# Clustered attention before two expert layers: cluster products on four column tiles, one assignment for both halves, the output halves added on GpSimd

## The chip, the core and the metric

One core of one Trainium2 chip. The metric is the device time of one execution in microseconds. TensorE (PE), VectorE (DVE), ScalarE (ACT) and GpSimd (POOL) run their own queues of instructions in order; SyncE (SP) issues most DMAs, one after another.

## The reference

Attention over 2 batches, 8 heads, 768 tokens and 64 channels, in which a query sees only the keys of its own cluster; then a layer of eight experts (1,536 tokens, 512 to 1024 to 512 channels), then a gated layer (512 to 1536 to 512).

```python
q_n = q / (np.linalg.norm(q, axis=-1, keepdims=True) + 1e-06)
c_n = centroids / (np.linalg.norm(centroids, axis=-1, keepdims=True) + 1e-06)
q_assign = np.argmax(np.einsum('bhsd,hcd->bhsc', q_n, c_n), axis=-1)
...
mask = q_assign[:, :, :, None] == k_assign[:, :, None, :]
scores = np.where(mask, scale * np.matmul(q, k.transpose(0, 1, 3, 2)), -1000000000.0)
attn = np.exp(scores - np.max(scores, axis=-1, keepdims=True))
attn = attn / (np.sum(attn, axis=-1, keepdims=True) + 1e-09)
return np.matmul(attn, v)
```

With 16 clusters, each token of q and k gets the first cluster with the largest product (the norm of the token changes no order). The change touches attention alone.

## The kernel before, in words

**Pairs and steps.** The 16 heads are taken as 8 pairs (two heads side by side in 128 partitions, 64 channels each). `Attention.run` walks 96 steps `g`, twelve to a pair; a step is 128 queries of one head against its 768 keys. The list `CFG["order"]` says in what order a step issues its parts: `E` (`evac`, in every third step: copy the finished output accumulator out), `S` (`soft`, the exponential of the next step), `Q` (`qk`, the score products of the step after that, and VectorE's maximum of them), `T0` and `T1` (`pt`: each three transposes of the exponentials, a ScalarE cast to the high part, a VectorE subtraction for the low part), `B0` (the first background part that falls to this step), `O` (`onat`, output products of a finished half), `V0` and `V1` (`pv`, two matmuls each on the high and two on the low parts into `acc`), `B1` (the other background parts). So on TensorE a step begins with the score products of two steps later. PSUM tiles: `s` and `t` have two buffers, `acc` and `mm` one; everything in the background and the output products share `mm`.

**Numbers in float32 precision.** The score products use float32r and split operands: q and k are transposed, cast to a high part H, the rest is a low part L (GpSimd or VectorE), and X = H + L is the exact value. SP moves H and L into the tiles A and B that the products read (`moves`, L181). The tiles B hold, beside the parts, 16 rows per head in which the one-hot cluster of each token stands, for the keys scaled by a large number, so that the score product itself adds the mask.

**The background of a pair.** While pair n-1 runs, pair n is prepared. `prep_steps` names the parts and `CFG["offs"]` (for the first prepared pair `CFG["offs1"]`) gives each a step, counted from the start of pair n-1; parts of one step keep the order of the list. Negative numbers lie in the pair before. Step 8: q0, 9: k0, 10: q1, 0: k1 (transposes `tr`, and behind the second half the moves), then the loads of the next pair. Step 2: v1, a0q. Step 3: a0k. Step 4: v0. Step 6: a1q, a1k, f0, f1. Step 7: m0, m1. The output products fall to steps 1 and 5, `evac` to steps 0, 3, 6 and 9.

**Assignment** (`assign`, L193; `first`, L219; for the first pair `assign0`). For each half of the tokens and each of q and k, three plain float32 matmuls have 128 tokens of X as the stationary operand and the 32 columns of two heads' centroids (`cbd`) as the moving one (L205); each appears in the trace as two records. When both are there, VectorE takes the maximum over the 16 clusters (L214), compares (L215), GpSimd multiplies by descending ranks (L216), and `first` takes the maximum of that and compares again (L226, L227): a one-hot of the first best cluster, tokens in partitions.

**Mask** (`mask`, L256). For each half the one-hot (128 x 64) is transposed by three matmuls (L266), ScalarE scales it into `oT` (64 rows: q and k of two heads, L280), and after the second half SP moves four blocks of 16 rows x 768 tokens into `qB` and `kB` (L131).

**Copy-out** (`evac`, L383). `acc` holds the product with V's high part in its lower 64 partitions and with V's low part in the upper ones: ScalarE copies the upper half (L391), VectorE adds it to the lower one into `O` (L393). The last pair takes its heads in another order, and its output product is in the same step as the copy-out.

Of the kernel before, what the change touches and what calls it, by code (L numbers as in the profile page):

```python
# [23 lines left out]
class Attention:  # L24


    def __init__(self, tc, ctx, q, k, v, cent, gate, x, lg, ident, raw):
# [23 lines left out]
        self.desc = one.tile([128, J * 2, C], F32, name="desc")  # L51
        self.sc = one.tile([4 * C, 2], F32, name="sc")
# [4 lines left out]
    def fixed(self):  # L57

        nc, C = self.nc, self.C
        nc.gpsimd.memset(self.cbd, 0.0)  # L60
        nc.gpsimd.memset(self.sc[0:2 * C, 0:1], 1.0)
        nc.gpsimd.memset(self.sc[0:2 * C, 1:2], 0.0)
        nc.gpsimd.memset(self.sc[2 * C:4 * C, 0:1], NEG)
        nc.gpsimd.memset(self.sc[2 * C:4 * C, 1:2], -NEG)
        nc.gpsimd.iota(self.desc, pattern=[[0, self.J * 2], [-1, C]], base=C, channel_multiplier=0,
                       allow_small_or_imprecise_dtypes=True)
        for t in self.qB + self.kB:
            nc.gpsimd.memset(t[0:64, 1, :].bitcast(F32), 0.0)
# [124 lines left out]
    def assign(self, n, half, si):  # L193
        nc, st = self.nc, self.pairs[n]
        J, C = self.J, self.C
        HJ = J // 2
        b, hp = divmod(n, self.H // 2)
        if si == 0:
            if half == 0:
                st["oh"] = self.one.tile([128, J, 4, C], F32, name="oh")  # L200
            st["ps"] = self.ps_m.tile([128, HJ, 4, C], F32, tag="mm", name="asp")
        ps = st["ps"]
# [5 lines left out]
        if si == 0:  # L208
            return
        G = HJ * 4  # L210
        psf = ps.rearrange("p j s c -> p (j s) c")
        mx = self.p2.tile([128, G], F32, name="mx")
        eq = self.p2.tile([128, G, C], F32, name="eq")
# [3 lines left out]
        st["eq", half] = eq  # L217

    def first(self, n, half):  # L219
        nc, st = self.nc, self.pairs[n]  # L220
        J, C = self.J, self.C
        HJ = J // 2
        G = HJ * 4
        eq = st.pop(("eq", half))
        m2 = self.p2.tile([128, G], F32, name="m2")
# [4 lines left out]
    def assign0(self, si):  # L230
# [3 lines left out]
        G = J * 2  # L234
# [961 lines left out]
```

## Time and profile before

| | |
|---|---|
| time, median of 3 runs | 815.84 us (815.63 to 816.18) |
| the profiled execution's own time | 816.51 us |
| its span, first to last instruction | 814.8 us |
| TensorE busy, granted clock | 786.3 us (97% of the span), 0.993 of full speed |
| VectorE, ScalarE, GpSimd busy | 597.6, 397.8, 263.3 us |
| attention's steps | from 15.35 us (first score product) to about 277 us |

The span leaves out 1.7 us around the first and the last instruction. Busy shares are averages over attention, experts and the gated layer, which have different limits: in attention VectorE and ScalarE are much busier than over the whole span, so the change is read from attention's own stretch. In timelines a row starts with its start and its duration in us; neighbouring instructions of one kind are one row (x2, x6), and records of one engine can overlap.

### The profile page before, as it was taken

Reading aid. Unit: us, or ns where it says so; the run is one execution under the profiler, and the core shown is the slowest. Engines: PE = TensorE matmul, PEld = TensorE weight load, DVE = VectorE, ACT = ScalarE, POOL = GpSimd, SP = SyncE. Lnnn points to the kernel's source line nnn. Section 1 sums busy time; section 2 is a strip of 40 time slices with the busy share of each in tenths; the row PEclk is TensorE's granted clock in tenths of the full one; section 3 lists DMA queues with packets and bytes.
Section 4 is the critical chain, followed back from the end, with each engine's and each line's share of the span. In section 5 each row is a group of like instructions: output and inputs, shape, how many; then the busy total and the mean of one; then the engine's idle time right before and its main releaser. Section 6 shows DMA issues by size and latency. Waiting matters only on the chain. (4 is left out here: it accounts for less than half of the span.)

```text
span 814.8 us, 13168 instructions
## 1 busy us (share of the span) xinstructions
PE 786.3 (97%) x4903; PEld 710.6 (87%) x4903; DVE 597.6 (73%) x995; ACT 397.8 (49%) x757; POOL 263.3 (32%) x283
## 2 busy tenths in 40 slices
PE   7999999999999889999999999999999999999996
PEld 6999999998989779999999988778888888888885
DVE  5899999999999757666565643678877777777433
ACT  5797887887988544455444532233322222212210
POOL 6322222322221285000000011566545445444234
PEclk9899999999999999999999999999999999999999
DMA  9855957725531166666664641322122121210012
GB/s 203 212 124 149 231 162 210 175 59 128 127 102 69 60 238 197 206 209 213 221 218 154 200 155 30 100 77 91 65 78 78 52 76 54 78 53 0 1 52 103
DMA packets 93316, 102.06 MB, mean 125 GB/s; under 512 B 30304, under 2 KB 77408, under 8 KB 93248
## 3 DMA queue, kind: packets, MB, share of 16 engines
q1 hardware_dynamic: 88384, 89.33, 38.3%
q0 software_dynamic: 1920, 6.29, 2.0%
q10 hardware_dynamic: 2944, 5.54, 1.9%
q8 instruction: 42, 0.69, 0.3%
q14 instruction: 26, 0.21, 0.1%
HBM read 68.21 MB, written 12.58 MB: 99 GB/s over the span
## 5 line engine op out<-in xcount | busy, mean ns | idle before, releaser
L366 DVE TENSOR_TENSOR PTl<-t,PTh 128x384 fp32r<-128x384 f32 x192 | 98.1, 548 | 6.2 <-ACT PTh L365 5.3
L1003 POOL TENSOR_TENSOR cm<-raw 128x512 f32<-128x512 f32 x36 | 47.8, 1329 | 155.6 <-DMA raw<-in_moe_w_gate 153.6
L365 ACT CAST PTh<-t 128x384 fp32r<-128x384 f32 x192 | 83.7, 491 | 27.6 <-PE t L363 27.3
L337 DVE TENSOR_REDUCE nm<-s 128x1 f32<-128x768 f32 x96 | 91.2, 951 | 6.7 <-PE s L334 5.7
L347 ACT ACTIVATE P<-s,nm 128x768 f32<-128x768 f32 x96 | 87.8, 914 | 2.7 <-DVE nm L337 1.7
L363 PE MATMUL t<-ident,P 128*128 128x128 f32 x576 | 83.2, 278 | 0.8 <-DVE PTl L366 0.7
L363 PEld LDWEIGHTS t<-ident,P 128*128 128x128 f32 x576 | 68.2, 142 | 9.7 <-DVE PTl L366 3.9
L380 PE MATMUL acc<-PTh,V 128*128 128x384 f32 x192 | 73.0, 380 | 1.3 <-DVE O L393 1.2
L841 PE MATMUL yp<-Hhh,W2h 128*128 128x256 f32 x256 | 73.1, 285 | 0.0
L1048 POOL TENSOR_TENSOR ghl<-u,ghh 128x512 fp32r<-128x512 f32 x36 | 49.8, 1384 | 71.4 <-ACT ghh L1047 71.4
L841 PE MATMUL hp<-Xl,W1h 128*128 128x256 f32 x256 | 72.6, 283 | 0.3 <-DVE Xl L834 0.3
L841 PE MATMUL hp<-Xh,W1h 128*128 128x256 f32 x256 | 72.6, 283 | 0.3 <-ACT Xh L833 0.3
L841 PE MATMUL yp<-Hhh,W2l 128*128 128x256 f32 x256 | 72.5, 283 | 0.0
L841 PE MATMUL yp<-Hhl,W2h 128*128 128x256 f32 x256 | 72.4, 283 | 0.0
L841 PE MATMUL hp<-Xh,W1l 128*128 128x256 f32 x256 | 72.4, 283 | 0.0
L380 PE MATMUL acc<-PTl,V 128*128 128x384 f32 x192 | 64.6, 337 | 0.0
L1045 DVE TENSOR_TENSOR u<-sg,g 128x512 f32<-128x512 f32 x36 | 24.8, 688 | 52.1 <-ACT sg L1044 52.1
L1067 DVE TENSOR_TENSOR acc<-o,acc 128x512 f32<-128x512 f32 x60 | 40.4, 690 | 19.7 <-PE o L1059 19.7
L334 PE MATMUL s<-Ak,Aq 128*128 128x384 f32 x192 | 52.6, 355 | 1.4 <-ACT P L347 1.4
L1047 ACT CAST ghh<-u 128x512 fp32r<-128x512 f32 x36 | 22.4, 621 | 64.3 <-DVE u L1046 64.3
L334 PE MATMUL s<-kB,qB 80*128 80x384 f32 (+1 forms) x192 | 50.7, 345 | 0.9 <-ACT kB L272 0.7
L808 DVE TENSOR_TENSOR W2l<-raw,W2h 128x1024 fp32r<-128x1024 f32 x32 | 40.0, 1249 | 15.1 <-ACT W2h L807 14.4
(268 smaller groups left out, 2137.9 us busy)
## 6 DMA issues: line engine op xcount, KB each, us to landing
raw<-in_moe_w SPq DMA_DIRECT2D x64, 512.0 KB, 4.4
Ak<-Hk SPq DMA_DIRECT2D x32, 192.0 KB, 4.9
moe_rows<-zero SPq DMA_DIRECT2D x8, 768.0 KB, 6.0
raw<-in_moe_w_gate SPq DMA_DIRECT2D x12, 512.0 KB, 3.6
raw<-in_moe_w_val SPq DMA_DIRECT2D x12, 512.0 KB, 3.6
raw<-in_moe_w_out SPq DMA_DIRECT2D x12, 512.0 KB, 3.5
xr<-moe_rows ACTq DMA_DIRECT2D x7, 768.0 KB, 6.4
ldq<-in_q SPq DMA_DIRECT2D x16, 192.0 KB, 4.2
```

Of the source, the lines that this page charges most:

```text
L334: nc.tensor.matmul(ps[:, c, 0:HS], lhsT=ql[:, qs], rhs=kr[:, c * HS:(c + 1) * HS], start=a == 0, stop=a == 1)
L337: nc.vector.tensor_reduce(out=nm, in_=ps[:, :, 0:HS], axis=AX.XY, op=ALU.max, negate=True)
L347: nc.scalar.activation(out=P, in_=ps[:, :, 0:HS], func=AF.Exp, bias=nm, accum_out=self.pairs[n]["sum"][:, i, r:r + 1])
L363: nc.tensor.transpose(ps[:, jj, :], P[:, a, jj * 128:(jj + 1) * 128], self.ident)
L365: nc.scalar.copy(out=Ph[:, js, cs], in_=ps)
L366: nc.vector.tensor_tensor(out=Pl[:, js, cs], in0=ps, in1=Ph[:, js, cs].bitcast(F32), op=ALU.subtract)
L380: nc.tensor.matmul(hs["acc"], lhsT=V[:, j, :], rhs=m[:, j, :], start=(j == 0 and a == 0), stop=(j == self.J - 1 and a == 1))
L808: nc.vector.tensor_tensor(out=l, in0=t, in1=h.bitcast(F32), op=ALU.subtract)
L841: self.nc.tensor.matmul(out, lhsT=W[a][:, k, cols], rhs=mov[b][:, k, :], start=i == 0, stop=i == n - 1)
L1003: self.nc.gpsimd.tensor_tensor(out=m, in0=Hw, in1=Hw, op=ALU.mult)
L1048: nc.gpsimd.tensor_tensor(out=hl[:, fc], in0=u, in1=hh[:, fc].bitcast(F32), op=ALU.subtract)
L1067: nc.vector.tensor_tensor(out=a, in0=p[t], in1=a, op=ALU.add)
```

## The change

The 12 cluster products of a pair become four: the centroids (32 columns) are stationary, 384 tokens of X move, and the four products (two halves, q and k) go to four column tiles of 32, so that their results stand in four blocks of 32 partitions of one PSUM tile (`assign`). ScalarE copies that to SBUF, and a new part `pick` transposes it by three matmuls back to tokens in partitions, where both halves are assigned at once (384 columns instead of twice 192). `mask` transposes the one-hot of both halves by three matmuls, one activation scales it, and eight moves of 16 rows x 384 tokens take it to B. The new tiles lie in the buffers of others (`as` in that of Lq, `eqa` in that of Lk). The parts a0q, a0k, a1q, a1k, f0, f1, m0, m1 become a, t, f, m, at steps 2, 3, 5, 7 (first prepared pair: 3, 4, 5, 6). In `evac` ScalarE copies both halves of the accumulator and GpSimd adds them. The ranks are kept once and broadcast; the first pair's own mask is now `mask0`.

```diff
-    def assign(self, n, half, si):
+    def assign(self, n):
...
-        for jj in range(HJ):
-            j = half * HJ + jj
-            nc.tensor.matmul(ps[:, jj, 2 * si:2 * si + 2].rearrange("p r c -> p (r c)"),
-                             lhsT=st["X" + "qk"[si]][:, j * 128:(j + 1) * 128], rhs=self.cbd[:, hp, :],
-                             start=True, stop=True)
...
+        ps = self.ps_m.tile([128, HS], F32, tag="mm", name="asp")
+        for half in range(2):
+            for si, nm in enumerate("qk"):
+                g = (2 * half + si) * 2 * C
+                nc.tensor.matmul(ps[g:g + 2 * C], lhsT=self.cbd[:, hp, :], rhs=st["X" + nm][:, half * HS:(half + 1) * HS],
+                                 start=True, stop=True, tile_position=(0, g))
+        st["as"] = self.one.tile([128, HS], F32, tag="Lq", name="as")
+        nc.scalar.copy(out=st["as"], in_=ps)
+
+    def pick(self, n):
...
+        ps = self.ps_m.tile([128, HJ, 128], F32, tag="mm", name="ast")
         for jj in range(HJ):
+            nc.tensor.transpose(ps[:, jj, :], st["as"][:, jj * 128:(jj + 1) * 128], self.ident)
+        G = HJ * 8
...
+        mx = self.one.tile([128, G], F32, name="mxa")
+        eq = self.one.tile([128, G, C], F32, tag="Lk", name="eqa")
         nc.vector.tensor_reduce(out=mx, in_=psf, axis=AX.X, op=ALU.max)
         nc.vector.tensor_tensor(out=eq, in0=psf, in1=mx.unsqueeze(2).to_broadcast([128, G, C]), op=ALU.is_equal)
-        nc.gpsimd.tensor_tensor(out=eq, in0=eq, in1=self.desc, op=ALU.mult)
+        nc.gpsimd.tensor_tensor(out=eq, in0=eq, in1=self.desc.to_broadcast([128, G, C]), op=ALU.mult)
...
+    def mask(self, n):
+        nc, st = self.nc, self.pairs[n]
+        C, HJ, HS = self.C, self.J // 2, self.S // 2
+        oT = self.one.tile([128, HS], F32R, tag="oT", name="oT")
+        ps = self.ps_m.tile([128, HJ, 128], F32, tag="mm", name="otp")
+        for jj in range(HJ):
+            nc.tensor.transpose(ps[:, jj, :], st["oh"][:, jj, :], self.ident)
+        nc.scalar.activation(out=oT, in_=ps.rearrange("p j t -> p (j t)"), func=AF.Identity, scale=self.sc[:, 0:1],
+                             bias=self.sc[:, 1:2])
+        for half in range(2):
+            sl = slice(half * HS, (half + 1) * HS)
+            for si, nm in enumerate("qk"):
                 Bt = st["B" + nm]
-                r0 = 2 * si * C
-                if n:
-                    self.move(Bt[64:64 + C, 0], st["oT"][r0:r0 + C])
-                self.move(Bt[64 - C:64, 1], st["oT"][r0 + C:r0 + 2 * C])
+                r0 = (2 * half + si) * 2 * C
+                self.move(Bt[64:64 + C, 0, sl], oT[r0:r0 + C])
+                self.move(Bt[64 - C:64, 1, sl], oT[r0 + C:r0 + 2 * C])
...
-        ol = self.one.tile([D, HS], F32, tag="ol", name="ol")
-        nc.scalar.copy(out=ol, in_=acc[D:2 * D])
-        o = self.pairs[n]["O"][r * D:(r + 1) * D, half * HS:(half + 1) * HS]
-        nc.vector.tensor_tensor(out=o, in0=acc[0:D], in1=ol, op=ALU.add)
+        rows = slice(r * D, (r + 1) * D)
+        ol = self.one.tile([2 * D, HS], F32, tag="ol", name="ol")
+        o = self.pairs[n]["O"][rows, half * HS:(half + 1) * HS]
+        nc.scalar.copy(out=o, in_=acc[0:D])
+        nc.scalar.copy(out=ol[rows], in_=acc[D:2 * D])
+        nc.gpsimd.tensor_tensor(out=o, in0=o, in1=ol[rows], op=ALU.add)
```

## Rows read from the trace of the kernel before

The pair shown is the fourth in order of time; its steps begin, on TensorE, at 110.58 (step 10 of the pair before it, by the score products that are two steps ahead), 112.99 (11), 115.05 (0), 117.58 (1), 120.49 (2), 123.13 (3), 125.95 (4), 128.02 (5), 130.83 (6), 134.15 (7), 137.65 (8), 140.12 (9), and 142.68 begins the next step 10.

**Rows 1.** Busy us (instructions) by stage: PE, PEld, DVE, ACT, POOL; clock, DMA, GB/s.
```profile
110.58:142.68 32.10, 31.66 (x223) 30.17 (x223) 29.98 (x60) 26.24 (x61) 8.19 (x10) 1.00 0.69 191
110.58:120.49 9.91, 9.91 (x70) 9.38 (x70) 9.34 (x17) 9.77 (x24) 3.02 (x3) 1.00 0.57 124
120.49:123.13 2.64, 2.64 (x21) 2.60 (x21) 2.50 (x8) 1.54 (x5) 0.35 (x1) 1.00 1.02 357
123.13:137.65 14.52, 14.08 (x102) 13.37 (x102) 13.60 (x29) 10.23 (x23) 3.80 (x6) 1.00 0.88 259
137.65:142.68 5.03, 5.03 (x37) 4.81 (x35) 4.55 (x9) 4.69 (x11) 1.00 (x1) 1.00 0.20 41
```

**Rows 2.** Timeline of TensorE: steps 11 and 0 begin, step 7's mask transposes.
```profile
112.99 0.52 PE L334 MATMUL s<-Ak,Aq 128*128 128x384 f32 x2
...
115.05 0.51 PE L334 MATMUL s<-Ak,Aq 128*128 128x384 f32 x2
...
136.13 0.49 PE L266 MATMUL otp<-ident,oh 128*64 128x128 f32 x3 [0.38 <-DVE oh L227]
```

**Rows 3.** Two source lines: duration ns min/median/max, first and last start.
```profile
L205 PE MATMUL asp<-cbd,Xq x84: 192/276/276, 29.1 to 230.2; 128*128 128x32 f32 x84
...
L410 PE MATMUL on<-R,O x96: 286/286/390, 54.8 to 280.2; 128*128 128x144 f32 x96
```

**Rows 4.** Groups, 30 to 320 us: busy us, mean ns | idle us before.
```profile
L366 DVE TENSOR_TENSOR PTl<-t,PTh 128x384 fp32r<-128x384 f32 x186 | 94.8, 548 | 5.6 <-ACT PTh L365 5.0
...
L337 DVE TENSOR_REDUCE nm<-s 128x1 f32<-128x768 f32 x90 | 85.6, 951 | 3.9 <-PE s L334 2.9
...
L347 ACT ACTIVATE P<-s,nm 128x768 f32<-128x768 f32 x91 | 83.3, 915 | 2.5 <-DVE nm L337 1.5
...
L391 ACT COPY ol<-acc 64x384 f32<-64x384 f32 x32 | 15.2, 477 | 10.7 <-PE acc L380 10.0 <-ACT x L662 0.2
...
L393 DVE TENSOR_TENSOR O<-acc,ol 64x384 f32<-64x384 f32 x32 | 17.5, 547 | 0.7 <-ACT ol L391 0.2
...
L280 ACT ACTIVATE oT<-otp,sc 64x384 fp32r<-64x384 f32 x14 | 9.4, 669 | 6.1 <-PE otp L266 6.1
...
L214 DVE TENSOR_REDUCE mx<-asp 128x12 f32<-128x192 f32 x14 | 5.0, 354 | 1.2 <-PE asp L205 1.0
...
L157 POOL TENSOR_TENSOR Lk<-Xk,Hk 128x384 fp32r<-128x384 f32 x12 | 12.0, 1003 | 25.9 <-ACT Xk L156 25.9
```

**Rows 5.** Timeline of ScalarE in step 3 and of VectorE in step 5.
```profile
124.45 0.86 ACT L365 CAST PTh<-t 128x384 fp32r<-128x384 f32 x2 [0.15 <-PE t L363]
...
130.73 0.16 DVE L405 TENSOR_SCALAR rs<-sum 128x6 f32<-128x6 f32 x1
...
131.82 0.54 DVE L393 TENSOR_TENSOR O<-acc,ol 64x384 f32<-64x384 f32 x1
```

**Rows 6.** Timeline of SP's DMA issues, two pairs.
```profile
124.86 0.60 SPq L131 DMA_DIRECT2D kB<-Lk  x1
...
138.63 1.22 SPq L131 DMA_DIRECT2D qB<-oT  x2
139.90 1.22 SPq L131 DMA_DIRECT2D kB<-oT  x2
...
238.26 1.22 SPq L131 DMA_DIRECT2D kB<-oT  x2
```

**Rows 7.** DMA issues by line: count, KB each, us from issue to landing.
```profile
kB<-Lk SPq DMA_DIRECT2D x16, 192.0 KB, 4.4
...
kB<-oT SPq DMA_DIRECT2D x15, 48.0 KB, 2.1
```

**Rows 8.** Timeline of TensorE: first score products of a new pair.
```profile
143.03 0.52 PE L334 MATMUL s<-kB,qB 80*128 80x384 f32 x2
...
239.87 0.51 PE L334 MATMUL s<-Ak,Aq 128*128 128x384 f32 x2
...
240.49 0.59 PE L334 MATMUL s<-kB,qB 80*128 80x384 f32 x2
```

More of the change, by code (lines that the diff above doesn't have):

```diff
@@ L50, in __init__ @@
         self.cbd = one.tile([128, H // 2, 2 * C], F32, name="cbd")
[L51 to L52 removed]
+        self.desc = one.tile([128, 1, C], F32, name="desc")
+        self.sc = one.tile([8 * C, 2], F32, name="sc")
         self.pairs = {}
@@ L214, in assign, with first @@
         nc.vector.tensor_reduce(out=mx, in_=psf, axis=AX.X, op=ALU.max)
         nc.vector.tensor_tensor(out=eq, in0=psf, in1=mx.unsqueeze(2).to_broadcast([128, G, C]), op=ALU.is_equal)
-        nc.gpsimd.tensor_tensor(out=eq, in0=eq, in1=self.desc, op=ALU.mult)
-        st["eq", half] = eq
-    def first(self, n, half):
+        nc.gpsimd.tensor_tensor(out=eq, in0=eq, in1=self.desc.to_broadcast([128, G, C]), op=ALU.mult)
+        st["eq"] = eq
+    def first(self, n):
         nc, st = self.nc, self.pairs[n]
[L221 to L225, printed above, removed]
+        C, HJ = self.C, self.J // 2
+        G = HJ * 8
+        eq = st.pop("eq")
+        m2 = self.one.tile([128, G], F32, name="m2a")
@@ L226, in first @@
         nc.vector.tensor_reduce(out=m2, in_=eq, axis=AX.X, op=ALU.max)
-        nc.vector.tensor_tensor(out=st["oh"][:, half * HJ:(half + 1) * HJ].rearrange("p j s c -> p (j s) c"), in0=eq,
+        st["oh"] = self.one.tile([128, HJ, 128], F32, tag="oh", name="oh")
+        nc.vector.tensor_tensor(out=st["oh"].rearrange("p j (g c) -> p (j g) c", c=C), in0=eq,
                                 in1=m2.unsqueeze(2).to_broadcast([128, G, C]), op=ALU.is_equal)
@@ L236, in assign0 @@
         if si == 0:
-            st["oh"] = self.one.tile([128, J, 4, C], F32, name="oh")
+            st["oh"] = self.one.tile([128, J, 4, C], F32, tag="oh", name="oh")
         pt = self.ps_t.tile([128, J // 2, 128], F32, tag="t", name="t")
@@ L254, in assign0, with mask0 @@
                         op=ALU.is_equal)
-    def mask(self, n, half):
-        nc, st = self.nc, self.pairs[n]
+    def mask0(self, half):
+        nc, st = self.nc, self.pairs[0]
         J, C, S = self.J, self.C, self.S
@@ new lines, in mask0 @@
+        nc.scalar.activation(out=st["Bk"][64:64 + C, 0, sl], in_=flat[2 * C:3 * C], func=AF.Identity,
+                             scale=self.sc[2 * C:3 * C, 0:1], bias=self.sc[2 * C:3 * C, 1:2])
+        self.late.append((sl, flat))
+        for sl, flat in self.late if half else ():
+            nc.vector.tensor_copy(st["oT"][q, sl], flat[q])
+            nc.scalar.activation(out=st["oT"][k, sl], in_=flat[k], func=AF.Identity, scale=self.sc[k, 0:1],
+                                 bias=self.sc[k, 1:2])
@@ L454, in run @@
         self.warm(self.ps_m, "mm", 28)
-        self.mask(0, 0)
-        self.mask(0, 1)
+        self.mask0(0)
+        self.mask0(1)
         self.vsplit(0, 0)
```

54 lines of the change are left out of this document (18 added, 36 removed).

## The prediction, made before the changed kernel ran

> **What bounds the kernel now.** I read the busy time by stage first, then TensorE's order of work, then the other engines' durations, last the DMA issues of SP. Attention runs in twelve steps to a pair of heads; seven of the eight pairs carry the preparation of the next pair, and only that preparation and the copy-out of the output change. The first view [rows 1] cuts one such pair (32.10 us) at its steps: steps 10, 11, 0 and 1 take 9.91, step 2 takes 2.64, steps 3 to 7 take 14.52, steps 8 and 9 take 5.03. TensorE is busy in 31.66 of the 32.10, VectorE in 29.98, ScalarE in 26.24, GpSimd in 8.19. So TensorE sets the pair, with VectorE close behind, and from step 8 to step 1 ScalarE too (4.69 + 9.77 of 14.94). A step without preparation takes 2.06 us, from one score product's start to the next [rows 2]. Twelve of those are 24.7 us; the other 7.4 are preparation, output products and waits. One wait is plain: in step 7 the transposes of the mask wait 0.38 us for VectorE's one-hot [rows 2].
>
> **The cluster products.** Before, a pair issues 24 records (two per product, 12 products, 128x32): 6 in step 2, which is why that step takes 0.58 more than a plain one, 6 in step 3 and 12 in step 6; some 2.4 us in all. After, it issues 8 records of 384 columns, all in step 2. Their price follows from two rows [rows 3]: a plain f32 record lasts 192 ns at its shortest with 32 columns and 286 with 144, so a column costs 94/112 = 0.84 ns (two cycles at the granted 2.4 GHz), and 384 columns stream for 0.32 us. No row has column tiles, so the sum has two ends: all 8 one behind the other are 8 x 0.32 = 2.6 us, and four tiles fully side by side are 2 x 0.32 = 0.64 us. Both records of a product need the same 32 columns of the array and have to follow each other; the program issues tile 0 twice, tile 1 twice and so on. If TensorE starts records in their order, the second record of one tile can run with the first of the next, and no more: five slots, 1.6 us. I take 1.7, with 0.1 for going in and out of the tiles. It lies between the ends, since the records of this trace all keep their order, which excludes the lower end, and the upper one would need the tiles to do nothing. The Trainium skill (TensorEngine Tiling (Array Packing), Key Properties) says that different tiles run their matmuls in parallel, but also that a change of tiling mode drains the engine; by the first alone the products would take 0.64 us, which is a rival below.
>
> Step 2 so goes from 2.64 to 2.06 + 1.7 = 3.76: **+1.1**.
>
> **Steps 3 to 7.** TensorE loses 18 records of products (6 in step 3, 12 in step 6) and 3 of 6 mask transposes, and gains 3 transposes of the copied scores in step 3 (128 columns, 0.11 each). Its own work there is then five plain steps, 0.33 for scores, 0.33 for the mask and 0.73 for one output product (6 records of 0.12): 11.7 us. VectorE loses two output additions (547 ns each), and its assignment turns from two sets of 192 columns into one of 384: a reduction goes from 354 ns to about 0.55 (between the 354 of 192 and the 951 of 768 columns), a 384-wide operation takes 548 [rows 4]; start to start the four come to 2.05 us, where the eight old ones took about 2.8. ScalarE loses one mask activation (669), and gains the score copy (about 0.48) and a second output copy for each group of three steps (477) [rows 4]. GpSimd's product with the descending ranks and its output sum are about 1.0 us each, as its 384-wide subtraction [rows 4]; with 24 idle us in a pair it hides both. The sum waits for ScalarE's copies; behind it in GpSimd's queue stand k's low part (step 0) and the product with the ranks (step 3), each some 1 us later and read a step later; the output products read the sum a step or more after it, but for the last pair.
>
> What counts is the order. The products end with step 2, so the score copy waits at the head of ScalarE's queue until then, and behind it are the two output copies and the exponential that step 4 needs. From the start of step 3: score copy 0.2 to 0.65, output copies to 1.6, exponential to 2.5 (915 ns), casts from 2.5. Before, the casts began at 1.3 (124.45 [rows 5], less 123.13). VectorE's first subtraction follows the cast by 0.5, at 3.0 instead of 1.9. From there its queue is nearly full: two subtractions to 4.0, maximum and equality to 5.05, step 4 to 6.85 (a plain step costs it 1.85, one maximum of scores and two subtractions, neighbours overlapping), step 5 to 8.65, the one-hot to 9.6, the output scaling to 10.7 (1.09, from its first record to the group after it [rows 5]), step 6's subtractions to 12.4. The transposes write a PSUM tile of two buffers, so those of step 7 can't start before step 6's subtractions release them, at 12.0 and 12.45; with mask transposes and output accumulation step 7 ends at 13.8 instead of 14.52: **-0.7**. The 2.1 us between this and TensorE's own 11.7 are new waits for VectorE; the old one for the one-hot is gone.
>
> One more wait can arise: the equality now writes into the buffer of Lk, whose last move is issued at 124.86 [rows 6] and lands 4.4 us later [rows 7], at about 129.3. In the new order the equality runs at 123.13 + 1.1 + 4.5 = 128.7. That is 0.6 at most, in the pairs whose queue also carries zero fills; I take it at nothing and keep it for the range.
>
> **Steps 8 to 1.** The accumulator is released by two ScalarE copies instead of a copy and an addition queued on VectorE; I give back 0.25 for the waits in steps 9 and 0. ScalarE gets 0.95 more work against 0.48 idle; the other 0.5 is hidden while TensorE waits in step 10 for the mask, and would show without that wait. That wait is the price. Before, SP issued four moves of the mask from 138.63 on, 0.63 apart [rows 6], and they land 2.1 us after issue [rows 7]; the third, issued at 139.90, lands at 142.0, and the product that reads it starts at 143.03 [rows 8]: 1.0 of slack. In a later pair the third is issued at 238.26 [rows 6], so lands at 240.4, and the product starts at 240.49, 0.62 behind its forerunner, where 0.35 is usual [rows 8]; so this wait exists already. After, there are eight moves of half the size, and the keys of the first head are complete only with the seventh. No row shows an issue get shorter with its rows, so I keep 0.63 for each: four issues or 2.54 us later. (Behind the moves SP has only those of q in step 10, which come free later than that.) Against it stand 0.68 (with one activation the first issue comes about 0.3 after step 8 begins, not 0.98), the slack of 1.0 and 0.18 because only the second matmul needs the seventh move: 0.7, and 0.85 as steps 8 and 9 are themselves 0.15 faster. Bounds: 0 if a half-size move issues in 0.4, 1.5 if the product waits for all eight. **+0.6** net.
>
> **The sum.** A middle pair: 1.1 - 0.7 + 0.6 = +1.0; six of them, +6.0. The first prepares its mask a step earlier and has no wait for it: +0.2. The last has no preparation and a relieved VectorE, but its one output product in the copy-out's own step now waits for two copies and a GpSimd sum: +0.3. Start-up and experts see nothing: four more small memsets and a shorter iota lie under the first loads. The profiled execution takes 816.51 us, 0.67 above the median; 816.51 + 6.5 - 0.67 = **822.3 us**.
>
> **Rivals.** (a) VectorE's relief decides: it loses about 2.9 us a pair, and if the lead of the score products covers its bursts in steps 3 and 5, a pair falls to TensorE's work, 24.7 + 1.3 + 1.5 for unchanged transposes and output products, 0.66 and 1.7 for the new ones, 29.9, plus the wait for the mask: 30.75. That is -1.35 in six pairs and some -2.4 for first and last: 805. The high busy share of VectorE speaks for it, the late casts of step 3 against; it decides if steps 4 to 7 hold no TensorE gap over 0.2 us. Chance 0.25. (b) Tiles truly side by side: 0.75 for the products, 0.95 less a pair, 815.7, no change. No row shows two records side by side. Chance 0.2. The Trainium skill stands on both sides (TensorE: Matmul & The Clock Gate, Part 3): it measured 2.38 times for three column tiles, yet calls matmuls strictly in order, as my five slots do; no run here shows either for tiles. (c) The tiles don't overlap at all, so the change doesn't do what it says: 2.7 for the products, 829. All matmul records here stream one by one. Chance 0.2. My case has 0.35.
>
> **Numbers.** Less than 0.2% (1.6 us) can't be told from no change here. Faster: (a) and a little of (b), 0.28. Same: half of (b) and an edge of mine, 0.14. Slower: 0.58. The range goes from 808, inside (a), to 829, the middle of (c); it leaves out the far half of each, about 0.2.
>
> **What would show it.** Right: 8 product records spread over some 1.6 us at the end of step 2; casts of step 3 about a microsecond later; TensorE waiting for subtractions in steps 4 to 7; a gap of 0.5 to 1.0 before the mask's second key product in step 10, ended by a move into kB. Wrong: a middle pair under 31.5 us, no gap in step 10, or products that take 0.7 or 2.6.

## The result, and the profile after the change

| | before | after |
|---|---|---|
| time, median | 816.63 us (815.63 to 817.91, 7 runs) | 827.22 us (822.19 to 828.22, 7 runs) |
| ratio | | 1.0107, 95% interval 1.0081 to 1.0134 |
| profiled execution, span | 816.51, 814.8 us | 824.82, 822.8 us |
| granted clock in it | 0.993 | 0.991 |
| first to 96th score product | 250.8 us | 257.2 us |

The change is slower, by 10.6 us in the medians (1.1%, with an interval clear of 1). Part of that is the clock: the granted clock differs between executions, and 4 of the 7 runs of after had 0.986 or 0.987. The one run of after at 0.996 took 822.19; three runs of before at 0.996, from all comparisons, took 815.29 to 815.52. So at equal clock the difference is 6.8 us, as far as one run of after can tell. In the two profiles it lies in attention's steps (6.4), in the stretch from the last score product to the first expert product, in which the last output products and the router stand (31.65 us after 31.07; below: the tail), and in TensorE's clock at start-up. After that the time is the same (517.5 us before and 517.3 after, from the first expert product to the end).

The clock at start-up belongs to the execution: in this profile of after TensorE was granted half its clock (1.2 of 2.4 GHz) for 3.41 us from 10.05 us, in the middle of nearly unbroken transposes and products, and its first score product came at 16.59 us; in the nine profiles of kernels below that have no such stretch it came at 15.25 to 15.66, as before the change (15.35), and in the three that have it at 16.27 to 16.42. A second such stretch, of 6.83 us, lies in the first pair, from 18.89 us before and from 20.29 after. So the comparisons below use **A**, the time from the 13th to the 96th score product, behind both: 219.72 us before, 226.62 after (its ends in after are the rows at 47.18 and 273.80 of the TensorE fence below). A pair is named by its place in order; the fourth is the one of [rows 1].

The fourth pair of after, by the same stages as [rows 1] (all, steps 10 to 1, 2, 3 to 7, 8 and 9; columns as there):

```profile
112.20:145.18 32.98, 31.34 (x208) 27.41 (x208) 27.33 (x50) 28.40 (x65) 11.94 (x14) 1.00 0.67 185
...
112.20:122.90 10.70, 10.21 (x69) 9.39 (x69) 8.63 (x15) 10.32 (x26) 4.53 (x5) 1.00 0.59 134
...
122.90:125.83 2.93, 2.93 (x23) 2.03 (x22) 2.79 (x9) 1.61 (x4) 0.56 (x2) 1.00 0.97 321
...
125.83:140.38 14.55, 13.40 (x86) 11.27 (x83) 12.28 (x25) 11.82 (x26) 5.40 (x6) 1.00 0.86 248
...
140.38:145.18 4.80, 4.80 (x36) 4.72 (x36) 3.63 (x6) 4.65 (x11) 1.45 (x2) 1.00 0.11 26
```

TensorE now has 15 records fewer, VectorE is 2.65 us less busy, ScalarE 2.2 and GpSimd 3.75 us more; and yet the pair is 0.88 longer, because TensorE idles for 1.64 us where it idled for 0.44. The stages say where: steps 10 to 1 take 0.79 more, step 2 takes 0.29 more, steps 3 to 7 the same, steps 8 and 9 take 0.23 less.

TensorE's timeline in after (start, duration, count, idle before): the wait in step 10, the products at the end of step 2, the wait in step 5, the last score product, the last pair's output product behind it.

```profile
47.18 0.52 PE L348 MATMUL s<-Ak,Aq 128*128 128x384 f32 x2
...
113.40 0.44 PE L348 MATMUL s<-kB,qB 80*128 80x384 f32 x1 [0.49 <-DMA kB<-oT]
...
124.78 0.34 PE L394 MATMUL acc<-PTl,V 128*128 128x384 f32 x1
125.05 0.51 PE L203 MATMUL asp<-Xq,cbd 128*32 128x384 f32 x1
125.06 0.51 PE L203 MATMUL asp<-Xk,cbd 128*32 128x384 f32 x1
125.06 0.51 PE L203 MATMUL asp<-Xq,cbd 128*32 128x384 f32 x1
125.07 0.51 PE L203 MATMUL asp<-Xk,cbd 128*32 128x384 f32 x1
125.40 0.49 PE L203 MATMUL asp<-Xq,cbd 128*32 128x384 f32 x1
...
125.42 0.49 PE L203 MATMUL asp<-Xk,cbd 128*32 128x384 f32 x1
125.83 0.62 PE L348 MATMUL s<-Ak,Aq 128*128 128x384 f32 x2
...
132.78 1.01 PE L377 MATMUL t<-ident,P 128*128 128x128 f32 x6 [0.85 <-DVE PTl L380]
...
273.80 0.52 PE L348 MATMUL s<-Ak,Aq 128*128 128x384 f32 x2
...
276.82 1.00 PE L426 MATMUL on<-R,O 128*128 128x144 f32 x6 [1.30 <-POOL O L409]
```

**The products run side by side.** The first records of all four tiles start within 0.02 us, the four second ones 0.35 later. From 124.96, where the next record would have followed (0.18 behind 124.78, as its neighbours), to the score product at 125.83 the four products cost TensorE 0.87 us. The column of the last record streams until about 125.74 (an estimate: 0.32 us for 384 columns, as in the prediction), so some 0.09 us are lost on the way into the tiles and 0.09 on the way out.

**ScalarE and VectorE in step 3**, which begins at 125.83 (timelines of after, ScalarE first):

```profile
126.01 0.48 ACT L206 COPY as<-asp 128x384 f32<-128x384 f32 x1 [1.02 <-PE asp L203]
126.52 0.47 ACT L407 COPY O<-acc 64x384 f32<-64x384 f32 x1
127.01 0.47 ACT L408 COPY ol<-acc 64x384 f32<-64x384 f32 x1
127.51 0.90 ACT L361 ACTIVATE P<-s,nm 128x768 f32<-128x768 f32 x1
...
128.40 0.85 ACT L379 CAST PTh<-t 128x384 fp32r<-128x384 f32 x2
```

```profile
128.90 1.02 DVE L380 TENSOR_TENSOR PTl<-t,PTh 128x384 fp32r<-128x384 f32 x2 [1.10 <-ACT PTh L379]
129.84 0.55 DVE L218 TENSOR_REDUCE mxa<-ast 128x24 f32<-128x384 f32 x1
130.84 0.56 DVE L219 TENSOR_TENSOR eqa<-ast,mxa 128x384 f32<-128x384 f32 x1 [0.45 <-DMA kB<-Lk]
131.32 0.94 DVE L351 TENSOR_REDUCE nm<-s 128x1 f32<-128x768 f32 x1
132.18 1.01 DVE L380 TENSOR_TENSOR PTl<-t,PTh 128x384 fp32r<-128x384 f32 x2
```

ScalarE idles 1.02 us for the products and then has two copies and an exponential ahead of the casts, which begin 2.57 us into the step. VectorE idles 1.10 us for them, then does its two subtractions, the maximum, waits 0.45 us for a move that still reads Lk, and is late with step 4's subtractions, for which TensorE waits 0.85 us in step 5.

**SP's mask moves** ahead of the same pair's step 10 (timeline of SP, then the profile's DMA list with count, KB each and us to landing):

```profile
107.68 1.22 SPq L132 DMA_DIRECT2D qB<-oT  x2
108.95 1.22 SPq L132 DMA_DIRECT2D kB<-oT  x2
110.21 1.22 SPq L132 DMA_DIRECT2D qB<-oT  x2
111.48 1.22 SPq L132 DMA_DIRECT2D kB<-oT  x2
```

```profile
kB<-oT SPq DMA_DIRECT2D x28, 24.0 KB, 1.9
```

A move of half the size still takes 0.63 us to issue. The seventh of the eight is issued at 111.48, and its reader starts at 113.40, 1.9 us later.

Summed over the pairs, the steps read: first pair -0.5, six middle pairs +5.13 (193.42 to 198.55), last pair +1.77 (26.30 to 28.07), tail +0.58: +7.0 in all. The six middle pairs are not alike: +0.2 in the second and the sixth, +0.7 and +0.9 in the third and the fourth, +1.3 in the fifth, +1.8 in the seventh. The seventh is taken up at kernels 4 and 5. In the fifth, one pair of move issues ahead of step 10 took 0.7 us more than any other in this profile:

```profile
142.04 1.94 SPq L132 DMA_DIRECT2D kB<-oT  x2
```

Step 10 waited 1.36 us there and lasted 4.04, against 3.1 to 3.3 in the fifth pairs of kernels 2, 3, 4 and 6, which wait for the same eight moves in the same order. So some 0.8 us of A in after belong to this one execution.

### The profile page after: what moved, and what is told of

It is laid out like the page before. It is cut to its first block, busy times and chain, and to the rows that moved or that the text cites. A ratio compares the mean times of both kernels' runs of the same rounds, so it can differ in the third digit from the quotient of the medians.

```text
span 822.8 us, 12991 instructions
## 1 busy us (share of the span) xinstructions
PE 785.7 (95%) x4791; PEld 693.4 (84%) x4791; DVE 577.2 (70%) x935; ACT 413.1 (50%) x789; POOL 293.2 (36%) x312
## 5 line engine op out<-in xcount | busy, mean ns | idle before, releaser
L377 PE MATMUL t<-ident,P 128*128 128x128 f32 x576 | 86.8, 282 | 7.4 <-DVE PTl L380 7.2
L409 POOL TENSOR_TENSOR O<-O,ol 64x384 f32<-64x384 f32 x32 | 32.2, 1006 | 55.3 <-ACT ol L408 53.3
```

Source lines behind the costliest of these rows:

```text
L377: nc.tensor.transpose(ps[:, jj, :], P[:, a, jj * 128:(jj + 1) * 128], self.ident)
```

## The experiments

Each kernel is after or before with the edit shown. The table has the medians, the ratio to runs of before on the same chip with its interval, A, the fourth pair and the last pair (to the 96th score product), all in us. The intervals of after and of 1 to 4 and 6 overlap, so these kernels are told apart by their steps, each from one profiled execution; two executions of kernel 9 agree in A within 0.1 us.

| kernel | median | ratio | A | 4th pair | last |
|---|---|---|---|---|---|
| before | 816.2 to 818.0 | | 219.7 | 32.10 | 26.30 |
| after | 827.2 | 1.0107 [1.0081, 1.0134] | 226.6 | 32.98 | 28.07 |
| 1 first head's moves first | 824.4 | 1.0086 [1.0059, 1.0114] | 224.1 | 33.00 | 27.28 |
| 2 one-hot in step 6 | 827.6 | 1.0111 [1.0071, 1.015] | 227.2 | 33.50 | 28.00 |
| 3 products before the rest of step 2 | 825.0 | 1.0106 [1.0067, 1.0144] | 225.3 | 32.96 | 28.04 |
| 4 old copy-out | 824.8 | 1.0098 [1.007, 1.0127] | 223.1 | 33.19 | 27.32 |
| 5 before with the new copy-out | 823.4 | 1.0086 [1.0051, 1.012] | 222.7 | 32.51 | 27.29 |
| 6 buffer of its own | 824.6 | 1.0078 [1.0049, 1.0107] | 225.0 | 32.58 | 28.04 |
| 7 three mended | 815.2 | 0.9956 [0.9933, 0.9978] | 217.8 | 31.76 | 26.02 |
| 8 all a step earlier | 820.7 | 1.003 [1.0014, 1.0047] | 222.6 | 32.41 | 26.02 |
| 9 maximum in step 2 | 810.6 | 0.9927 [0.9904, 0.995] | 213.8 | 30.98 | 26.03 |
| 10 one-hot in step 4 | 813.5 | 0.9959 [0.9942, 0.9977] | 217.2 | 31.52 | 26.01 |
| 11 as 9, new copy-out | 815.5 | 0.9959 [0.9937, 0.998] | 215.4 | 31.03 | 27.29 |
| 9 again | 811.1 | 0.9932 [0.9909, 0.9955] | 213.7 | 30.98 | 26.03 |

### 1. The first head's moves first

```diff
-        for half in range(2):
-            sl = slice(half * HS, (half + 1) * HS)
-            for si, nm in enumerate("qk"):
...
-                self.move(Bt[64:64 + C, 0, sl], oT[r0:r0 + C])
-                self.move(Bt[64 - C:64, 1, sl], oT[r0 + C:r0 + 2 * C])
+        for r in range(2):
+            for half in range(2):
+                sl = slice(half * HS, (half + 1) * HS)
+                for si, nm in enumerate("qk"):
+                    r0 = (2 * half + si) * 2 * C + r * C
...
+                    self.move(st["B" + nm][rows, r, sl], oT[r0:r0 + C])
```

> Only the order of the mask's eight moves is other: the four of the first head first, then the four of the second. Theory A (the wait for the mask in step 10 is SP's row of eight issues at 0.63 us, of which the product needs the seventh): now it needs the fourth, 1.9 us earlier, so step 10 of the middle pairs goes back from 3.1 to 2.4 us and the time falls by 0.7 to 0.8 in five of them and 1.6 in the slowest, 4 to 5.5 us in all. Theory B (TensorE waits there because the other engines are late after steps 3 to 7, and the move is only the last thing seen): step 10 stays above 2.8 or the wait comes back in step 11 or 0; under 1.5 us in all.

A is 2.5 us shorter, of which some 0.8 is the slow issue in the fifth pair of after; theory A had 4 to 5.5. In the fourth pair step 10 fell from 3.16 to 2.68 and the wait for the mask is gone; in the last pair, where nothing else is prepared, the whole gain stays: 28.07 to 27.28. In the middle it does not always: the fourth pair is still 33.00, because step 5 went from 4.01 to 4.44. TensorE comes to step 2 sooner, Lk's move lands when it did, and VectorE waits longer for it. Waits of VectorE, 45 to 235 us (total, times, longest), in this kernel, then in after:

```profile
DVE PTl L380 <- ACT PTh L379: 20.3, 30, 1.1
...
DVE eqa L219 <- DMA kB<-Lk: 1.5, 2, 0.9
```

```profile
DVE eqa L219 <- DMA kB<-Lk: 0.8, 2, 0.5
```

So the wait for the mask is SP's row of issues, as theory A says, but what it gives back is partly waited for in step 5.

### 2. The one-hot in step 6

```diff
-['f', 5], ['k1', 0]], 'xe'
+['f', 6], ['k1', 0]], 'xe'
```

> Only the one-hot part f is other: in step 6 instead of step 5. Theory A (VectorE gets maximum, comparison and the output scaling in a row in step 5, so that step 7's transposes wait for its subtractions): steps 5 to 7 of a middle pair fall from 9.3 to about 8.9, since the burst of 2.1 us is split in two, less a wait of the mask's transposes for the one-hot of up to 0.4; 2 to 3 us in all. Theory B (the late casts of step 3 set VectorE back and it stays back until step 8): no change within 0.1 us a pair.

Step 5 kept its length (3.64 to 3.91 in pairs 2 to 6, where after has 3.65 to 4.01), and step 7 grew from 3.07 to 3.58, since the mask's transposes now wait for the one-hot. So theory A falls: the one-hot is not what makes step 5 wait. The pair is 0.5 longer, which neither theory had.

### 3. The products before the rest of step 2

```diff
-'offs': [['q1', -2], ['q0', -4], ['v1', 2], ['k0', -3], ['m', 7], ['v0', 4], ['a', 2],
+'offs': [['q1', -2], ['q0', -4], ['a', 2], ['v1', 2], ['k0', -3], ['m', 7], ['v0', 4],
```

> Only the order of two parts of step 2 is other: the cluster products run before the output accumulation of that step, not after it. Theory A (the score copy holds ScalarE's queue until the products are done, and with it the output copies, the exponential and the casts of step 3): the copy starts 0.7 us earlier, the casts of step 3 too, and the waits of steps 4 and 5 shrink by 0.5 to 0.7 us a pair, 3 to 5 us in all. Theory B (VectorE's own load in steps 3 to 5 sets those waits): casts earlier, but steps 3 to 7 the same within 0.2 us.

The casts of step 3 so begin 2.09 us into the step instead of 2.57, but that is only because step 2 is longer: steps 2 to 4 moved about among themselves (2.93, 2.73, 2.51 became 3.36, 2.40, 2.35: 8.17 to 8.11), and from the start of step 2 the casts come after 5.45 us instead of 5.50. The score copy does start earlier (2.71 us after the start of step 2 instead of 3.11), but ScalarE then waits 0.37 us for the accumulator before the output copies. So the edit did not make the casts earlier, and theory A is not tested by it; step 5 stayed at 4.02. Of the 1.3 us in A 0.8 is the fifth pair's step 10 (4.04 to 3.28), the slow issue of after.

### 4 and 5. The copy-out undone, and alone

```diff
...
-        nc.scalar.copy(out=o, in_=acc[0:D])
-        nc.scalar.copy(out=ol[rows], in_=acc[D:2 * D])
-        nc.gpsimd.tensor_tensor(out=o, in0=o, in1=ol[rows], op=ALU.add)
...
+        nc.scalar.copy(out=ol, in_=acc[D:2 * D])
...
+        nc.vector.tensor_tensor(out=o, in0=acc[0:D], in1=ol, op=ALU.add)
```

(4 is after with this edit; 5 is before with its reverse.)

> The copy-out is that of the kernel before (ScalarE copies one half, VectorE adds it to the other), the rest is the changed kernel. Theory A (the second ScalarE copy and the GpSimd sum cost more than VectorE's addition does): the last pair goes back from 28.1 to about 26.5, and in the middle pairs steps 0, 3, 6 and 9 gain on ScalarE what VectorE loses: a middle pair within 0.3 us of the changed kernel, 1.5 to 3 us faster in all. Theory B (the relief of VectorE is worth more than ScalarE's copies): middle pairs 0.5 to 1 us slower, the whole 2 us or more slower than the changed kernel.

> The kernel before with the new copy-out alone (two ScalarE copies, sum on GpSimd). Theory (the two halves of the change cost separately): undoing the copy-out in the changed kernel took its attention from 257.2 to 253.8 us, so adding it here should cost about as much: 819 to 819.5 us, with the last pair 0.8 to 1.8 longer than its 26.3 (the output product waits for GpSimd) and the mask's step or a router instruction of VectorE with two operands in SBUF longer in one pair. Rival 1 (the copy-out costs only beside the new assignment, because both press on ScalarE and VectorE in steps 3 to 5): within 0.8 us of before, 816.2. Rival 2 (VectorE's relief pays once the assignment is not lumped): below 815.

The copy-out costs by itself: A falls by 3.5 when it is undone (some 2.7 without the slow issue of after's fifth pair) and rises by 3.0 when it is added to before, so both rivals of 5 fall. The median of 5 is above what was expected (823.4, not 819 to 819.5); its profiled execution, at the clock of before's (0.993), took 820.96 against 816.51, 4.45 more, of which A holds 3.0 and the tail 0.6. It shows in three places. In the middle pairs of 5 step 10 is 2.85 instead of 2.41: the second copy stands ahead of step 10's exponential and casts on ScalarE, and TensorE's transposes wait for the subtractions behind them. Waits of TensorE's weight loads, 45 to 235 us, in 5 (before has 1.0 in 6 waits):

```profile
PEld t L363 <- DVE PTl L366: 4.6, 23, 0.3
```

In the last pair, which prepares nothing, it is again ScalarE: TensorE's score products wait 1.3 us in 4 waits for exponentials and its transposes 2.3 us for subtractions (before: none and 0.9), and the pair is 1.0 longer. In the tail the output product waits for GpSimd's sum, 1.65 us in 5 and 1.30 in after, where before the transposes waited 0.73 us near this place. And small VectorE instructions of the router are held up. The same instruction in after and in 4 (groups by form, 45 to 245 us: busy, mean ns):

```profile
L645 DVE TENSOR_TENSOR rt<-rlo,rmx 128x24 f32<-128x24 f32 x2 | 1.6, 824 | 0.0
```

```profile
L643 DVE TENSOR_TENSOR rt<-rlo,rmx 128x24 f32<-128x24 f32 x2 | 0.3, 170 | 0.0
```

One of the two in after took 1.48 us, and it ended when the GpSimd sum beside it did, within 0.06 us (timelines of VectorE and GpSimd in after):

```profile
236.68 1.48 DVE L645 TENSOR_TENSOR rt<-rlo,rmx 128x24 f32<-128x24 f32 x1
```

```profile
237.09 1.01 POOL L409 TENSOR_TENSOR O<-O,ol 64x384 f32<-64x384 f32 x1
```

That sum had stood behind two indirect DMAs in GpSimd's queue. VectorE's maximum and subtractions stand behind the held instruction, and TensorE's transposes wait for them (timeline of TensorE in after):

```profile
239.55 1.01 PE L377 MATMUL t<-ident,P 128*128 128x128 f32 x6 [1.75 <-DVE PTl L380]
```

So step 7 of that pair, the seventh, takes 4.59 us in after, where pairs 2 to 5 have 3.06 to 3.08 and the seventh of 4 has 2.41, as its neighbours. In 2, where the sum and the instruction do not meet, the instruction takes 0.17 us and the seventh pair's step 7 is as long as the others': this cost is a matter of how the two queues happen to fall.

Theory A of 4 had a last pair of 26.5 and 1.5 to 3 us; the last pair kept 1.0 of its excess, which is its wait for the mask (kernels 1 and 7). Undoing the copy-out did not simply give 3.5 us to the middle pairs: the fourth pair of 4 is 33.19. There TensorE's accumulation waits in step 6 for VectorE's addition instead (PE acc for DVE O, 5.3 us in 5 waits), and VectorE waited longer for Lk (1.9 us in 3 waits). What it gave lies in the last pair (-0.75), step 7 of the seventh pair (-2.2) and steps 4 and 7 elsewhere; step 10 of the fifth pair (-0.86) is the slow issue and not the copy-out.

### 6. A buffer of its own for the compared scores

```diff
-        eq = self.one.tile([128, G, C], F32, tag="Lk", name="eqa")
+        eq = self.one.tile([128, G, C], F32, tag="oT", name="eqa")
```

> The changed kernel with the compared scores in the mask's buffer instead of that of Lk, which SP's moves still read. Theory (the equality waits for Lk's last move to land, and that wait sits in VectorE's queue ahead of step 5's subtractions): step 5 is 3.65 us in every pair instead of 3.65 to 4.1, which is 1.1 us less over the pairs of the profiled execution, and no wait of VectorE for a move into kB is left; 826. Rival (the subtractions of step 5 are late for VectorE's own load alone): step 5 stays at 3.65 to 4.1, 827.

(The mask's buffer is idle from the end of its moves to step 7.) Step 5 is 3.57 to 3.60 in pairs 2 to 5 and 3.58 in the fourth, where it was 4.01; no wait of VectorE for a move into kB is left. The theory is right: step 5 is 1.0 us less over the six middle pairs, where 1.1 was expected. Of the 1.6 us in A half is step 10 of the fifth pair (4.04 to 3.18), the slow issue of after; that is not this buffer's.

### 7. Three mended

The edits of 1, 4 and 6 together, on after.

> The changed kernel with three things mended together: the four moves of the first head first, the old copy-out, and the mask's buffer for the compared scores. If the three costs add up (attention 257.2 less 2.9, 3.4 and 1.1, each from its own run or trace), attention takes 249.8 us against 250.8 before, and the time is 815 to 819. Rival (VectorE bounds steps 3 to 7 whatever else is mended, so what is saved ahead of step 5 is waited for in it): step 5 or 6 grows by what step 10 saves, attention stays over 252 and the time over 819.

A is 8.9 us under after, more than the sum of the single gains (2.5 + 3.5 + 1.6 = 7.6), and 2.0 us under before; from the first to the 96th score product it is 248.4 us, where 249.8 was expected. The slow issue of after's fifth pair is in all three single gains and only once in the joint one; without it the single gains are about 5 and the joint one 8. The time is 0.9956 of before. So the three costs more than add up, and each that was left hid part of the others' gain: the steps of the fourth pair are 2.39, 2.07, 2.46, 2.90, 2.96, 2.60, 2.21, 3.59, 3.37, 2.40, 2.40, 2.41. Steps 10, 11 and 0 are those of before, step 7 is 1.1 less than before, step 5 still 0.78 more.

### 8, 9 and 10. When the assignment happens

All three are 7 with `as` in the buffer of the one-hot instead of Lq's, and other steps in `offs` (`a` products, `t` transposes with maximum and equality, `f` one-hot, `m` mask); in 8 an empty part `z` pushes the products to the end of step 1.

```diff
 8
-['v1', 2], ['k0', -3], ['m', 7], ['v0', 4], ['a', 2], ['t', 3], ['f', 5], ['k1', 0]]
+['z', 1], ['a', 1], ['v1', 2], ['t', 2], ['k0', -3], ['m', 6], ['f', 4], ['v0', 4], ['k1', 0]]
 9
+['a', 2], ['v1', 2], ['t', 2], ['k0', -3], ['m', 6], ['f', 4], ['v0', 4], ['k1', 0]]
 10
+['v1', 2], ['a', 2], ['t', 3], ['k0', -3], ['m', 6], ['f', 4], ['v0', 4], ['k1', 0]]
```

> The kernel with the three things mended, and for all pairs but the first prepared one the whole assignment a step earlier: products at the end of step 1, transposes, maximum and equality at the end of step 2, one-hot in step 4, mask in step 6; so that no step holds two additions to VectorE's queue and the mask's moves are issued a step sooner. Theory (VectorE's additions, bunched in steps 3 to 5, set the wait in step 5): steps 2 to 7 lose 1 us or more against the run with the three mended, no pair has a step 5 over 3.2, step 10 has no wait for a move into kB, attention takes 243 to 247 and the time is 810 to 814. Rival (ScalarE, busy nearly throughout from step 8 to step 1, takes the score copy worse there than in step 3): the gain comes back as waits in steps 1 and 2, attention over 249, time within 2 us of the run with the three mended.

Step 1 became 5.12 us, 2.2 more than in 7: 0.87 for the products and the rest a wait, which ate the gain. The timeline of TensorE in 8 names a wait that neither theory had:

```profile
122.00 0.48 PE L203 MATMUL asp<-Xq,cbd 128*32 128x384 f32 x1 [1.27 <-DVE x L428]
```

The products share the PSUM buffer `mm` with the output product of step 1, and that is free only when VectorE has scaled the output. Steps 2 to 7 took 15.60 us against 17.13 in 7, but 0.87 of that is the products, which only moved to step 1; the rest, some 0.7, goes with step 5, which fell from 3.59 to 2.81. There was no wait in step 10. So the theory was right about step 5, and its 1 us or more was not reached; the rival's attention (over 249: 252.9 from first to 96th) came, but not for its reason.

> As the run one step earlier, but the products stand after step 2's transposes, behind the release of the shared buffer by the output scaling, and the transposes of the scores with maximum and equality at the end of step 2; one-hot in step 4, mask in step 6. In the run one step earlier the products waited 1.27 us in step 1 for VectorE's scaling of the output, while its steps 2 to 7 took 15.6 us against 17.1 with the three mended. If VectorE's bunched additions were the rest of the cost, step 1 is 2.9 again, steps 3 to 7 stay near 13.2 (14.2 with the three mended), step 2 is 3.0 to 3.5 as the transposes there follow the score copy closely, a middle pair takes 31.0 to 31.4 and the time is 811 to 813.5. Rival (the score copy and the transposes in one step make TensorE wait for ScalarE): step 2 is over 3.9 and the pair no shorter than 31.76.

Right in its mechanism: step 1 is 2.91, step 2 is 3.32, steps 3 to 7 take 13.03; the pair, 30.98, and the time, 810.6 (0.9927 of before), lie just under their ranges. The fourth pair by the stages of [rows 1] (all, step 2, steps 3 to 7), and VectorE from the end of step 2 on:

```profile
107.35:138.33 30.98, 30.14 (x208) 27.92 (x208) 29.19 (x55) 26.30 (x62) 7.97 (x9) 1.00 0.72 193
...
117.16:120.48 3.32, 3.32 (x27) 2.45 (x26) 2.98 (x8) 1.80 (x5) 0.02 (x1) 1.00 0.99 330
120.48:133.51 13.03, 12.19 (x82) 11.27 (x81) 12.48 (x24) 10.59 (x24) 3.93 (x5) 1.00 0.84 220
```

```profile
120.76 0.56 DVE L218 TENSOR_REDUCE mxa<-ast 128x24 f32<-128x384 f32 x1 [0.48 <-PE ast L213]
121.35 0.56 DVE L219 TENSOR_TENSOR eqa<-ast,mxa 128x384 f32<-128x384 f32 x1
121.94 0.55 DVE L407 TENSOR_TENSOR O<-acc,ol 64x384 f32<-64x384 f32 x1
122.52 0.96 DVE L351 TENSOR_REDUCE nm<-s 128x1 f32<-128x768 f32 x1
123.39 1.01 DVE L380 TENSOR_TENSOR PTl<-t,PTh 128x384 fp32r<-128x384 f32 x2
```

Here maximum and equality fill the time in which VectorE would wait for ScalarE; in 7 the addition of the copy-out waited 1.06 us for ScalarE's copy at that point (timeline of VectorE in 7), and maximum and equality came after step 3's subtractions:

```profile
124.66 0.55 DVE L407 TENSOR_TENSOR O<-acc,ol 64x384 f32<-64x384 f32 x1 [1.06 <-ACT ol L405]
```

> As the run with the three mended, but the one-hot in step 4 and the mask in step 6; products at the end of step 2 and maximum and equality in step 3 stay. If it is the sum of VectorE's additions up to step 5 that makes step 5 wait, steps 3 and 4 together with step 5 stay at 8.4 and only step 6 changes, a pair is 31.4 to 31.8 and the time 814 to 816. If it is the pair of additions inside step 5 itself (one-hot and output scaling), step 5 falls under 3.1, a pair to 31.0 or less and the time to 811 or 812.

The first branch: step 5 stayed at 3.59 (3.59 in 7), a pair is 31.52, the time 813.5, just under its range. Together with 2 this says that the one-hot may stand before, in or behind step 5; what step 5 waits for is maximum and equality in step 3. Two other differences between 10 and 9 remain: the products' place within step 2, which left step 5 as it was in 3, and the casts of step 3, which come 0.6 us earlier into the step in 9. They are not the reason: VectorE's first subtraction of that step comes 0.3 us later in 9 (at 123.39 in the rows above, 2.9 us into the step) than in 10 (2.6), and step 5 is still shorter in 9.

### 11. The new copy-out in the best version

Kernel 9 with the `evac` of after.

> The fastest version so far (products and maximum in step 2, one-hot in step 4, mask in step 6, 810.6 us against 816.9 before), but with the change's copy-out on two ScalarE copies and GpSimd. Theory (the copy-out costs by itself: ScalarE's second copy stands ahead of the exponential and the casts in its full steps, GpSimd's sum blocks an output product in the last pair and small operations of VectorE): as much slower as in the other two pairs of kernels, 3 us of attention, so 813 to 817, with a middle pair 0.3 to 0.6 longer and the last pair 1.0 longer. Rival (with VectorE's other work spread, TensorE's only long wait is for the accumulator, 2.9 and 4.6 us from step 0 to 11 of six pairs for VectorE's addition, which the new copy-out takes away): a middle pair of 30.4 or less and 806 to 810.

The time fell in the theory's range, but its mechanism only half: the last pair is 1.26 longer (1.0 expected), but the fourth pair only 0.05. TensorE's wait for the accumulator is gone, as the rival had it, and a wait for subtractions takes its place. Waits of TensorE's weight loads, 45 to 235 us, in 9 and in 11:

```profile
PEld t L377 <- DVE PTl L380: 0.8, 5, 0.2
```

```profile
PEld t L377 <- DVE PTl L380: 8.4, 40, 0.7
```

In A 1.6 us are lost, of the 3 expected. The medians lie 4.4 apart (815.5 and 811.1); the profiled execution of 11 had half clock for 10.2 us after attention and that of 9 for 3.4, but whether that explains the rest was not settled.

> The fastest version once more, beside the same runs of the kernel before: 809 to 812.5 us if the gain holds.

This is the repeat of 9 (despite the run's name, the kernel is 9's). It gave 811.1, ratio 0.9932: the gain holds.

## Why the prediction was right or wrong

The sign came out, +7.0 us in the steps against a forecast of +6.5, and the range held the time. Of its three mechanisms, VectorE being late and the mask being late came; the products' five slots did not. That the sum is so near is luck: two terms were missed by 0.8 and 0.7 a pair in opposite directions, two small ones (last pair and tail) by 2 us together, the first pair by 0.7 the other way, and 0.8 of the middle pairs' +5.13 is the one slow issue. By the forecast's own signs the products, at 0.87 us, lie nearer to "wrong" (0.7) than to "right" (1.6 spread out); the late casts, TensorE's wait for subtractions and the gap in step 10 came as listed.

**The cluster products: +1.1 forecast, +0.29 measured.** This step failed. "If TensorE starts records in their order ... five slots, 1.6 us": all four tiles start one after another within 0.02 us, and the second records 0.35 us later. The price is near the lower bound (0.64) plus some 0.2 for going in and out: 0.87, not 1.7. Rival (b) had this mechanism; that the time did not stay at 815.7, as it said, is due to the other terms. By the Trainium skill (TensorEngine Tiling (Array Packing), Key Properties) tiles run in parallel and a change of mode drains the engine; the trace agrees with the first, and leaves at most 0.09 us each way for the second.

**Steps 3 to 7: -0.7 forecast, 0.0 measured.** The queue of ScalarE and VectorE was forecast well: casts at 2.5 us into step 3 (2.57), first subtraction at 3.0 (3.07), maximum at 4.0 (4.01). The step that failed is "I take it at nothing" for Lk's move: in the fourth pair the equality waited 0.45 us, and everything behind it on VectorE was that late. With its own buffer (kernel 6) the five steps take 14.14, so -0.4 of the -0.7 is there. The wait stands in two of the six middle pairs (0.8 us together); the second and the fifth, without it, take 14.20 in after and 14.53 before. The rest shows in step 5, where the two new instructions of step 3 make VectorE late; that wait was named. That VectorE's idle time just ahead, 1.10 us, would have room for them was not seen.

**Steps 8 to 1: +0.6 forecast, +0.56 measured.** Right, and shown by kernel 1: eight moves of 24 KB issue at 0.63 us each, as those of 48 KB did, and the wait ends with the seventh. Its sum inside was not quite as told: step 10 took 0.75 more, of which 0.27 stayed when the moves were reordered; that is ScalarE's second copy (with the old copy-out as well, in 7, step 10 is 2.39), which the forecast called hidden "while TensorE waits in step 10", and named as showing without that wait.

**The last pair: +0.3 forecast, +1.77 measured.** Two omissions: it waits for its mask as the others do (step 10 3.27 instead of 2.40; kernel 1 gives 0.79 back), and ScalarE's second copy costs it 1.0 in its own steps (kernel 5). The wait forecast, that of the output product for two copies and a GpSimd sum, exists, but it stands in the tail.

**The first pair: +0.2 forecast, -0.5 measured; the tail: 0 forecast, +0.58.** The first pair holds a stretch of half clock in both profiles and was not followed up; kernel 9's took 29.97 us with 3.41 us of half clock in it and 28.71 without. The tail comes from the copy-out: 31.35 to 31.75 us in the seven kernels that have the new one, 30.94 to 31.29 in the seven executions with the old one. The output product's wait for GpSimd and two held-up VectorE instructions (below) stand in it; which weighs more was not told apart.

**Rival (a)**, that VectorE's relief decides, was wrong for the change as it is. Kernel 9 shows what it takes: with maximum and equality in VectorE's idle time and the rest mended, a pair takes 30.98. That this is near the rival's 30.75 is chance: 9 has the old copy-out, so less relief for VectorE, and no wait for the mask, which the rival's sum has. **Rival (c)** fell with the first records of the four tiles.

## What to carry to other kernels

- Less work on an engine gains nothing by itself: here VectorE was 2.65 us less busy in a pair that was 0.88 longer. Find the moment when its queue idles, and put the new piece there. Maximum and equality ahead of step 3's subtractions instead of behind them took 0.5 to 1.0 us off five of the six middle pairs (10 to 9).
- When a change has several parts, mend each cost alone and all together: alone, a saved wait was taken up by the next (1: -0.48 in step 10, +0.43 in step 5 of the fourth pair), together they turned +1.1% into -0.4%, and the placement into -0.7%.
- Count small moves, and issue first what is read first: eight half-size moves took 5.1 us to issue where four took 2.5.

## What the runs showed of the hardware

- Four float32 products of 384 columns on four column tiles of 32 take 0.87 us with the way in and out: eight records in two rounds 0.35 us apart, the four of a round some 0.007 us apart.
- A VectorE instruction with two operands in SBUF was held while GpSimd added two tiles in SBUF: 1.48 us instead of 0.17 for 24 columns (0.41 of it before the addition began, beside an indirect DMA of GpSimd), and in the router 0.93 and 0.90 instead of 0.16 for 3 columns. The first of these and the addition beside it end within 0.02 us of each other (timelines in after):

```profile
282.99 0.93 DVE L653 TENSOR_TENSOR ret<-ret,dump 128x3 f32<-128x3 f32 x1
```

```profile
282.89 1.01 POOL L409 TENSOR_TENSOR O<-O,ol 64x384 f32<-64x384 f32 x1 [6.13 <-ACT ol L408]
```

VectorE's subtractions, which read one operand from PSUM, were not held up (1.0 us for two beside GpSimd's instructions, as alone). The Trainium skill says the same (GPSIMD Engine Reference, Specifications): GpSimd shares its SBUF interfaces with VectorE and contends with instructions that have two SBUF inputs. So moving an addition to GpSimd was not free for VectorE.

- TensorE's granted clock fell from 2.4 to 1.2 GHz for 3.41 or 6.83 us at a time: in the first pair in 12 of the 14 profiles (before: from 18.89 us, behind waits of 0.66 us for the mask and while the next score products waited 1.37 us for an exponential), in four of them also before the first score product, in nine behind attention, each time shortly behind a wait of TensorE of 1.6 to 2.3 us; in other executions, as in that of before, such a wait (1.89 us) brought no fall. A difference of a few us between single executions can be this alone, and was told apart here by steps that begin after the first pair.
